# RWKV attention ahead of two expert layers on one Trainium2 core: attention tiles taken in pairs from tile 8 on

## The chip, the cores and the metric

The kernel runs on one core of a Trainium2 chip. The metric is the device time of one execution in microseconds (us); the kernel before and the changed one are compared by the median of their runs.

## The reference

Three layers follow each other. The first is a recurrence over 768 time steps (4 batches, 8 heads, head size 48), the other two are expert layers over 3072 tokens of 384 features.

```python
for t in range(S):
    cur = np.einsum('bhd,bhe->bhde', u[None] * kt, vt)
    y[:, :, t] = np.einsum('bhd,bhde->bhe', rt, state + cur)
    state = w[None, :, :, None] * state + np.einsum('bhd,bhe->bhde', kt, vt)
...
h = np.maximum(np.maximum(x @ w1, x @ w2), x @ w3); x = h @ w_out
...
silu(xn @ w_gate) * (xn @ w_val) @ w_out      # xn: x by its root mean square
```

## The kernel before, in words

**Tiles and stages.** The recurrence is worked in 24 attention tiles: tile i is 128 time steps of one batch (i % 4), 8 heads at once. Four tiles make one block of 512 tokens, the width of an expert matmul. The program is a list of stages `u` = 0 to 5 (the loop `for u in range(NB)`); stage u runs the first expert layer on block u and beside it the attention of block u+1, so tiles 8 to 11 belong to stage 1. A stage is a row of slots: in stages 1 to 4 there are 18 slots of `a_l1` (nine matmuls of 128x512, three each for three weight parts; after the slot VectorE takes a maximum, L537, or ScalarE a copy, L534) and 6 of `a_out` (nine matmuls). Stage 0 has 30 slots.

**One attention tile** is: `prep` (L321, VectorE multiplies the tile `raw` by decay tables; two products `ru`, from tile 8 on by GpSimd), `prep_b` (L337, a sum on VectorE; L340, GpSimd makes the diagonal matrix `Dg`), `pe_a` (L357, 16 matmul records into two PSUM banks `pa`), `mix` (L364, two predicated copies on VectorE from `pa` into `Dg`), `pe_y` (L431, the outputs `py`), `fin` (L446 and L447 split `py` into two halves of a float, from tile 8 on partly through a tile `yt` that `turn` moves between partitions with four DMAs), `pe_st` (L395, `pkv`) and `state` (L375 and L380). The profile counts matmuls of 4-byte numbers as several records.

**Order of the work.** Each engine takes its instructions in the order in which the program issues them. `att_steps` yields 72 steps for the attention. The slot loop issues a slot, then the work put off by the slot before (`later`), then as many steps as `want` asks, evenly over the slots; then `tick` issues pieces of the weights' conversion (L137 to L140 on ScalarE, L147 and sums L168 on VectorE). Up to tile 11 a step is `(scores(i + 1), outputs(i))`, that is `pe_a` and `mix` of the next tile and then `pe_y`, `fin`, `pe_st` of this one, followed by `ahead` (with `prep`) and `ahead_b` (with `prep_b`) of tile i+2. From tile 12 on `outputs` and `scores` each take two tiles at once, in different steps.

**PSUM.** The attention's banks come from the pool `psx`: four banks, given out in turn, each of which must be read before it is given out again. A tile takes four (two `pa`, `py`, `pkv`), a pair seven (four `pa`, two `py`, one `pkv`). One more is taken in stage 1: behind slot 8 `decay_flag` (L301 to L310) issues a small matmul `psok` (L305), whose result on VectorE says whether the decay is in range.

Of the kernel before, what the change touches and what calls it, by code (L numbers as in the profile page):

```python
# [56 lines left out]
FREE = (0, 2, 4, 4, 5, 5, 7, 10, 10)  # L57
TURN = (1, 0, 3)
TURNED = 8
DM, FF1, FF2 = 384, 768, 1536  # L60
NB = S // 128
NT = B * NB
# [9 lines left out]
def rwkv_moe_kernel(ctx, tc, rkT, rkv, wd, ub, cst, rg, w1p, wo1p, w2p, out):  # L72
# [173 lines left out]
    def load_next(n=1):  # L246
        for _ in range(n):
            if loads:
                loads.pop(0)()

    def load_tile(i):
        if i >= NT:
            return
        a = raws[i % 3][:, :, 0:512].rearrange("p s (q t) -> p s q t", t=128)
        t = tp.tile([128, VO + NP * 144], F32, tag="tm", bufs=3, name=f"tm{i}")
        raw_t[i], tm_t[i] = a, t
        for j in range(2):
            loads.append(lambda j=j: sync.dma_start(a[64 * j:64 * j + 48], rkT[i, 48 * j:48 * j + 48]))
        rk = t[:, 0:2 * KO].rearrange("p (s n) -> p s n", s=2)[:, :, 0:DM]
        loads.append(lambda: sync.dma_start(rk, rkv[i, :, 0:2 * DM].rearrange("p (s n) -> p s n", s=2)))  # L260
        loads.append(lambda: sync.dma_start(t[:, VO:], rkv[i, :, 2 * DM:]))
# [61 lines left out]
    def prep(i):  # L323
        prep_raw(i)
        s = st[i]
        tm = s["tm"]
        ru = tp.tile([128, DM], F32, tag="ru", name=f"ru{i}")
        eng = dve if i < NRU else pool
        eng.tensor_tensor(out=ru, in0=tm[:, 0:DM], in1=usb, op=ALU.mult)
        eng.tensor_tensor(out=ru, in0=ru, in1=tm[:, KO:KO + DM], op=ALU.mult)  # L330
        s["ru"] = ru

    def prep_b(i):
        s = st[i]
        a8 = tp.tile([128, H], F32, tag="a8", bufs=2, name=f"a8{i}")
        ru = s["ru"]
        dve.tensor_reduce(out=a8, in_=ru.rearrange("p (h d) -> p h d", d=D), op=ALU.add,  # L337
                          axis=mybir.AxisListType.X)
        Dg = tp.tile([128, H, 128], F32, tag="Dg", bufs=2, name=f"Dg{i}")
        pool.affine_select(out=Dg, in_=a8.unsqueeze(2).to_broadcast([128, H, 128]),  # L340
                           pattern=[[0, H], [1, 128]], channel_multiplier=-1, base=0,
                           compare_op=ALU.is_equal, fill=0.0)
        s["Dg"] = Dg

    def prep2(i):
        if i // B < NB - 1:
            k = st[i]["tm"][:, KO:KO + DM]
            pool.tensor_tensor(out=k, in0=k, in1=kt, op=ALU.mult)

    def pe_a(i):  # L350
        s = st[i]
        raw = s["raw"]
        pa = [psx.tile([128, NP, 128], F32, tag="x", name=f"pa{i}_{j}") for j in range(2)]
        for pr in range(NP):
            for j in range(2):
                sl = slice(64 * j, 64 * j + 48)
                pe.matmul(pa[j][:, pr], raw[sl, 1, pr], raw[sl, 0, pr], start=True, stop=True)  # L357
        s["pa"] = pa

    def mix(i):  # L360
        s = st[i]
        dg = s["Dg"].rearrange("p (r j) t -> p r j t", j=2)
        for j in range(2):
            dve.copy_predicated(out=dg[:, :, j], mask=cmask.unsqueeze(1).to_broadcast([128, NP, 128]),  # L364
                                data=s["pa"][j])
# [17 lines left out]
    def pe_st(i, pk=None):  # L383
        s = st[i]
        c, b = divmod(i, B)
        if c == NB - 1:
            return
        tm = s["tm"]
        v3 = tm[:, VO:].rearrange("p (r q e) -> p r q e", q=3, e=D)
        if pk is None:  # L390
            pk = psx.tile([128, NP, D], F32, tag="x", name=f"pkv{i}")
        for pr in range(NP):
            for j in range(2):
                o = KO + 96 * pr + 48 * j
                pe.matmul(pk[64 * j:64 * j + 64, pr], tm[:, o:o + 64], v3[:, pr, 2 * j], start=True, stop=True)  # L395
        s["pk"] = pk

    def state(i):
        c, b = divmod(i, B)
        if c == NB - 1:  # L400
            return
        pk = st[i]["pk"]
        decay(i)
        if i >= B:
            later.append(lambda: state_in(i, pk))
        else:
            state_in(i, pk)

    def pe_y(i):
        s = st[i]  # L410
        c, b = divmod(i, B)
        tm = s["tm"]
        py = s["py"] = psx.tile([128, 3, 128], F32, tag="x", name=f"py{i}")
        lanes = []
        for n in range(4):
            lane = []
            for k in range(3):
                m = (n + TURN[k] * (i >= TURNED)) % 4
                pr, o = (k, 32 * m) if m < 3 else (3, 32 * k)
                ops = [(tm[:, VO + 144 * pr + 48 * j + o:VO + 144 * pr + 48 * j + o + 32],  # L420
                        s["Dg"][:, 2 * pr + j]) for j in range(2) if o != (64, 0)[j]]
                if c > 0:
                    ops.append((Tst[b][:, pr, o:o + 32], s["raw"][:, 0, pr]))
                for m, (l, r) in enumerate(ops):
                    lane.append((py[32 * n:32 * n + 32, k], l, r, m == 0, m == len(ops) - 1))
            lanes.append(lane)
        for m in range(max(map(len, lanes))):
            for lane in lanes:
                if m < len(lane):
                    o, l, r, start, stop = lane[m]  # L430
                    pe.matmul(o, l, r, start=start, stop=stop)  # L431
# [3 lines left out]
    def fin(i):  # L435
        s = st[i]
        u, m = divmod(i, B)
        if m == 0:
            xt[u] = ap_.tile([128, 2, 3, 512], F32R, tag="x", bufs=2, name=f"x{u}")
        xh, xl = xt[u][:, 0], xt[u][:, 1]  # L440
        o = 128 * m
        cs = slice(o, o + 128)
        y = s["py"]

        def split(hi, lo, y):
            act.copy(hi, y)  # L446
            dve.tensor_tensor(out=lo, in0=y, in1=r32(hi), op=ALU.subtract)  # L447

        if i < TURNED:
            split(xh[:, :, cs], xl[:, :, cs], y)  # L450
            return
        t = tp.tile([128, 2, 2, 128], F32R, tag="yt", bufs=2, name=f"yt{i}")
        split(t[:, 0], t[:, 1], y[:, 0::2])
        split(xh[:, 1, cs], xl[:, 1, cs], y[:, 1])

        def turn():
            for n, k in enumerate((0, 2)):
                o = 32 * TURN[k]
                sync.dma_start(r32(xt[u][o:128, :, k, cs]), r32(t[0:128 - o, :, n]))
                sync.dma_start(r32(xt[u][0:o, :, k, cs]), r32(t[128 - o:128, :, n]))  # L460

        turns.append(turn)
# [3 lines left out]
    def att_steps():  # L466
        def scores(*tiles):
            for i in tiles:
                pe_a(i)
            for i in tiles:  # L470
                mix(i)

        def outputs(*tiles):
            for i in tiles:
                pe_y(i)
            for i in tiles:
                fin(i)
            pk = None
            if len(tiles) > 1 and tiles[0] // B < NB - 1:
                pk = psx.tile([128, 2, NP, D], F32, tag="x", name=f"pkv{tiles[0]}")  # L480
            for n, i in enumerate(tiles):
                pe_st(i, pk if pk is None else pk[:, n])
            for i in tiles:
                state(i)
                load_tile(i + 3)

        def ahead(i):
            while turns:
                turns.pop(0)()
            if i < NT:  # L490
                load_next(2)
                prep(i)

        def ahead_b(i):
            if i < NT:
                load_next(1)
                prep_b(i)
                prep2(i)

        for i in range(11):  # L500
            yield lambda i=i: (scores(i + 1), outputs(i))
            yield lambda i=i: ahead(i + 2)
            yield lambda i=i: ahead_b(i + 2)
        yield lambda: outputs(11)
        yield lambda: ahead(13)
        yield lambda: (ahead_b(13), scores(12, 13))
        for i in range(12, NT, 2):
            yield lambda i=i: (outputs(i, i + 1), load_next(2))
            for j in (i + 2, i + 3):
                yield lambda j=j: ahead(j)  # L510
                yield lambda j=j: ahead_b(j)
            yield lambda i=i: scores(i + 2, i + 3) if i + 2 < NT else None
# [845 lines left out]
```

## Time and profile before

| | us |
|---|---|
| median of 3 runs (809.25 to 812.47) | 811.64 |
| profiled execution | 809.68 |
| its span, first to last instruction | 808.0 |
| TensorE busy in the span | 789.1 |
| VectorE busy in the span | 563.9 |
| ScalarE busy in the span | 420.5 |
| GpSimd busy in the span | 215.3 |

The span is what the trace covers; the profiled execution is 1.7 us longer, for what lies around it. PE in the rows is TensorE, DVE VectorE, ACT ScalarE, POOL GpSimd, SP the engine that issues most DMAs. The mean granted clock of TensorE is 0.993 of full speed. Matmuls overlap, so the distance between the starts of two rows tells what a piece costs, not the duration that a row gives.

### The profile page before, as it was taken

What the parts mean: (1) busy time and instruction counts of PE and PEld (TensorE: products, weight loads), DVE (VectorE), ACT (ScalarE), POOL (GpSimd) and SP (SyncE); (2) the same over time, 40 slices, a digit from 0 to 9 for tenths busy, and PEclk for the clock granted to TensorE, in tenths of its full rate; (3) what the DMA queues carried; (4) which work ended last, traced back from release to release, by engine and by line L of the source; (5) the groups of instructions that cost most, each with busy time, mean ns of one, the idle gap of its engine ahead of it and who ended that gap; (6) DMA issues with size and microseconds to landing.
All of it is one profiled execution on the core that took longest, in us unless ns stands there. A gap on an engine that the chain in (4) does not pass through costs nothing.

```text
span 808.0 us, 14049 instructions
## 1 busy us (share of the span) xinstructions
PE 789.1 (98%) x5090; PEld 651.6 (81%) x5090; DVE 563.9 (70%) x981; ACT 420.5 (52%) x780; POOL 215.3 (27%) x225
## 2 busy tenths in 40 slices
PE   7899999999999999999999999999999999999996
PEld 6788888888888888888788888788888788888885
DVE  8888968749959749418846679856676874655551
ACT  2988864454454452224576675655444555444431
POOL 2486724333533322014368672000000000000000
PEclk9999999999999999999999999999999999999998
DMA  8986786666667733244289874328454405554211
GB/s 236 309 255 183 233 246 203 192 208 204 181 194 220 215 129 94 66 155 144 82 275 331 280 239 154 116 75 278 139 181 138 140 17 175 159 154 139 77 40 43
DMA packets 83738, 139.28 MB, mean 172 GB/s; under 512 B 10566, under 2 KB 47046, under 8 KB 83660
## 3 DMA queue, kind: packets, MB, share of 16 engines
q1 hardware_dynamic: 79964, 121.97, 49.9%
q0 software_dynamic: 3200, 15.73, 5.0%
q8 instruction: 42, 0.69, 0.4%
q10 hardware_dynamic: 496, 0.59, 0.3%
q14 instruction: 36, 0.29, 0.1%
HBM read 98.65 MB, written 35.41 MB: 166 GB/s over the span
## 4 chain that ended last, share of the span: by engine, by line
PE 94%; DVE 2%; ACT 2%; DMA 1%; issue 0%; POOL 0%; SPq 0%; POOLq 0%
PE px L99 11%; PE px L100 11%; PE px L101 11%; PE pl L99 9%; PE pl L100 9%; PE pl L101 9%; PE pa L100 5%; PE pa L101 5%; PE pa L99 5%; PE py L431 5%; PE po L99 3%; PE po L101 3%; PE po L100 3%; PE pa L357 3%; PE pkv L395 1%; PE pw L639 1%
## 5 line engine op out<-in xcount | busy, mean ns | idle before, releaser
L99 PE MATMUL pl<-x,w_a 128*128 128x512 f32 (+1 forms) x342 | 131.7, 385 | 0.3 <-ACT x L446 0.3
L100 PE MATMUL pl<-x,w_a 128*128 128x512 f32 (+1 forms) x342 | 129.6, 379 | 0.7 <-DVE x L447 0.7
L101 PE MATMUL pl<-x,w_a 128*128 128x512 f32 (+1 forms) x342 | 129.5, 379 | 0.5 <-POOL w_a L156 0.5
L99 PEld LDWEIGHTS pl<-x,w_a 128*128 128x128 f32 x342 | 64.3, 188 | 13.7 <-ACT x L446 0.9
L101 PEld LDWEIGHTS pl<-x,w_a 128*128 128x128 f32 x342 | 64.3, 188 | 13.0 <-POOL w_a L156 0.8
L100 PEld LDWEIGHTS pl<-x,w_a 128*128 128x128 f32 x342 | 64.3, 188 | 12.6 <-DVE x L447 1.1
L537 DVE TENSOR_TENSOR c<-pl,c 128x512 f32<-128x512 f32 (+1 forms) x76 | 50.0, 657 | 32.7 <-PE pl L101 30.7
L1076 DVE TENSOR_TENSOR px<-px,sb 128x512 f32<-128x512 f32 x56 | 39.1, 699 | 33.0 <-PE px L101 31.5
L539 ACT CAST h1h<-c 128x512 fp32r<-128x512 f32 (+1 forms) x32 | 19.0, 595 | 75.4 <-DVE c L537 75.3
L340 POOL TENSOR_SCALAR_AFFINE_SELECT Dg<-a 128x1024 f32<-128x1024 f32 x24 | 29.2, 1216 | 96.8 <-DVE a L337 79.2
L1064 ACT COPY sb<-px 128x512 f32<-128x512 f32 x63 | 37.0, 587 | 34.2 <-PE px L101 30.5
L700 POOL TENSOR_TENSOR ws<-wsf,ws 128x384 fp32r<-128x384 f32 x40 | 42.3, 1058 | 37.7 <-ACT ws L699 31.0
L100 PE MATMUL px<-hb,wo 128*128 128x512 f32 x132 | 51.5, 391 | 0.2 <-DVE hb L1062 0.2
L99 PE MATMUL px<-hb,wo 128*128 128x512 f32 x132 | 51.6, 391 | 0.0
L101 PE MATMUL px<-hb,wo 128*128 128x512 f32 x132 | 51.4, 389 | 0.0
L147 DVE SCALAR_TENSOR_TENSOR wf<-wf,wraw 128x384 uint32<-128x384 uint32 x60 | 42.4, 711 | 6.4 <-ACT wraw L140 6.0
L137 ACT ACTIVATE wf<-wraw 128x384 f32<-128x384 f32 x60 | 33.4, 557 | 14.7 <-DMA w2o<-wf 8.8
L431 PE MATMUL py<-Dg,tm 128*32 128x128 f32 x768 | 40.4, 287 | 0.0
L1100 DVE TENSOR_TENSOR hb<-h,hb 128x512 fp32r<-128x512 f32 x36 | 24.9, 692 | 21.8 <-ACT hb L1099 21.6
L139 ACT ACTIVATE wraw<-wraw 128x384 uint16<-128x384 uint32 x60 | 38.8, 647 | 1.9
L140 ACT ACTIVATE wraw<-wf 128x384 f16<-128x384 f32 x60 | 38.7, 646 | 1.9
L431 PEld LDWEIGHTS py<-Dg,tm 128*32 128x32 f32 x768 | 33.7, 114 | 4.5 <-issue 2.9
(306 smaller groups left out, 2063.7 us busy)
## 6 DMA issues: line engine op xcount, KB each, us to landing
ws<-w2s SPq DMA_DIRECT2D x80, 384.0 KB, 3.1
w2s<-ws POOLq DMA_DIRECT2D x40, 384.0 KB, 3.8
wraw<-in_w2p SPq DMA_DIRECT2D x36, 384.0 KB, 6.3
raw<-in_rkT SPq DMA_DIRECT2D x48, 192.0 KB, 4.7
tm<-in_rkv SPq DMA_DIRECT2D x24, 384.0 KB, 4.6
wsf<-w2f SPq DMA_DIRECT2D x120, 64.0 KB, 3.4
tm<-in_rkv SPq DMA_DIRECT2D x24, 288.0 KB, 5.1
wraw<-in_w1p SPq DMA_DIRECT2D x18, 384.0 KB, 7.0
```

What stands on the lines that cost most here:

```text
L99: pe.matmul(o, lh, rh, start=start, stop=False, **kw)
L100: pe.matmul(o, lh, rl, start=False, stop=False, **kw)
L101: pe.matmul(o, ll, rh, start=False, stop=stop, **kw)
L137: act.activation(w, hi.bitcast(F32), AF.Copy, scale=2.0 ** -112)
L139: act.activation(x[:, :, 0], lo, AF.Copy, scale=2.0 ** -29 * (1 - 2.0 ** -12), bias=-0.4996)
L140: act.activation(x[:, :, 1].bitcast(F16), w, AF.Copy)
L147: dve.scalar_tensor_tensor(out=wu, in0=wu, scalar=3, in1=cbits(n).bitcast(U32), op0=ALU.logical_shift_left, op1=ALU.bitwise_or)
L431: pe.matmul(o, l, r, start=start, stop=stop)
L537: dve.tensor_tensor(out=c1[:, :n], in0=p[:, :n], in1=c1[:, :n], op=ALU.max)
L700: pool.tensor_tensor(out=t[:, :, 1], in0=r, in1=r32(t[:, :, 0]), op=ALU.subtract)
L1064: (act.copy if kind == "e" else dve.tensor_copy)(get(ks[1]), get(ks[0]))
L1076: dve.tensor_tensor(out=o, in0=a, in1=b, op=op)
```

## The change

The number 12, from which tiles go in pairs, becomes a constant `PAIRED` = 8, and the three places that were written for 12 follow from it. Tiles 8 and 9 and tiles 10 and 11 are now pairs. The number of steps stays 72 and the slots in which steps are issued stay; only what a step holds is other.

```diff
+PAIRED = 8
...
-        for i in range(11):
+        for i in range(PAIRED - 1):
             yield lambda i=i: (scores(i + 1), outputs(i))
             yield lambda i=i: ahead(i + 2)
             yield lambda i=i: ahead_b(i + 2)
-        yield lambda: outputs(11)
-        yield lambda: ahead(13)
-        yield lambda: (ahead_b(13), scores(12, 13))
-        for i in range(12, NT, 2):
+        yield lambda: outputs(PAIRED - 1)
+        yield lambda: ahead(PAIRED + 1)
+        yield lambda: (ahead_b(PAIRED + 1), scores(PAIRED, PAIRED + 1))
+        for i in range(PAIRED, NT, 2):
             yield lambda i=i: (outputs(i, i + 1), load_next(2))
```

**TensorE at the end of stage 0.** Before, the scores of tile 9 (`pa9`) stand in stage 1, behind its first slot (`pl1_0_0`) and ahead of the outputs of tile 8:

```order
L99 MATMUL pl1_0_0_0_1382<-x1_704,w_a0_290 128x512
L100 MATMUL pl1_0_0_0_1382<-x1_704,w_a0_290 128x512
L101 MATMUL pl1_0_0_0_1382<-x1_704,w_a0_290 128x512
L357 MATMUL pa9_0_1394<-raw0_95 128x128 [waits DMAHW2_49,PE_49]
L357 MATMUL pa9_1_1395<-raw0_95 128x128 [waits DMAHW4_49,PE_49]
L357 MATMUL pa9_0_1394<-raw0_95 128x128
```

Now they stand in stage 0, behind those of tile 8 and ahead of the second slot of the output product (`po0_1`, five slots before stage 1):

```order
L358 MATMUL pa8_0_1240<-raw2_97 128x128
L358 MATMUL pa8_1_1241<-raw2_97 128x128
L358 MATMUL pa9_0_1250<-raw0_95 128x128 [waits DMAHW2_49,DVE_49,PE_49]
L358 MATMUL pa9_1_1251<-raw0_95 128x128 [waits DMAHW4_49,PE_49]
L358 MATMUL pa9_0_1250<-raw0_95 128x128
L358 MATMUL pa9_1_1251<-raw0_95 128x128
L358 MATMUL pa9_0_1250<-raw0_95 128x128
L358 MATMUL pa9_1_1251<-raw0_95 128x128
L358 MATMUL pa9_0_1250<-raw0_95 128x128
L358 MATMUL pa9_1_1251<-raw0_95 128x128
L100 MATMUL po0_1_1271<-h1h0_376,w_o0_1037 128x512 [waits Activation_49]
```

Six slots earlier, `pa9` names a wait for VectorE (DVE) that it did not need to name before. The scores of tile 8 moved from three slots earlier, where they stood ahead of the outputs of tile 7, to this place.

**TensorE in stage 1, at the flag's matmul.** Before, `psok` stands between two slots (`pl1_2_2` and `pl1_3_0`):

```order
L99 MATMUL pl1_2_2_0_1678<-x1_704,w_a2_495 128x512
L100 MATMUL pl1_2_2_0_1678<-x1_704,w_a2_495 128x512
L101 MATMUL pl1_2_2_0_1678<-x1_704,w_a2_495 128x512
L305 MATMUL psok_1695<-small_87,csb_85 1x4 [waits DVE_49]
L305 MATMUL psok_1695<-small_87,csb_85 1x4
L99 MATMUL pl1_3_0_0_1702<-x1_704,w_a3_623 128x512 [waits Activation_49]
```

Now the scores of tiles 10 and 11 stand between that slot and `psok`:

```order
L358 MATMUL pa11_0_1692<-raw2_97 128x128
L358 MATMUL pa11_1_1693<-raw2_97 128x128
L358 MATMUL pa11_0_1692<-raw2_97 128x128
L358 MATMUL pa11_1_1693<-raw2_97 128x128
L306 MATMUL psok_1706<-small_87,csb_85 1x4 [waits DVE_49]
L306 MATMUL psok_1706<-small_87,csb_85 1x4
L100 MATMUL pl1_3_0_0_1713<-x1_704,w_a3_623 128x512 [waits Activation_49]
```

The pool's turn now gives `psok` the bank that held `pa10_0`, the first of the four banks that were just written.

**VectorE at the same place.** Before, the sum of tile 11 and the flag's reduction (`nok`) come behind the two maxima of the slots:

```order
L537 TENSOR_TENSOR c11_2_0_1633<-pl1_2_1_0_1667,c11_2_0_1633 128x512 [waits PE_49,Activation_49]
L537 TENSOR_TENSOR c11_2_0_1633<-pl1_2_2_0_1678,c11_2_0_1633 128x512 [waits DVE_49,PE_49]
L337 TENSOR_REDUCE a811_1690<-ru11_1645 128x8 [waits Pool_49]
L307 TENSOR_REDUCE nok_1698<-psok_1695 1x1 [waits PE_49]
L309 CAST okflag_1700<-nok_1698 1x1 [waits DVE_49]
```

Now the four copies of `mix` for tiles 10 and 11 stand there:

```order
L538 TENSOR_TENSOR c11_2_0_1633<-pl1_2_1_0_1659,c11_2_0_1633 128x512 [waits PE_49,Activation_49]
L538 TENSOR_TENSOR c11_2_0_1633<-pl1_2_2_0_1670,c11_2_0_1633 128x512 [waits DVE_49,PE_49]
L365 COPY_PREDICATED Dg10_1574<-csb_85,pa10_0_1682 128x4x128 [waits PE_49]
L365 COPY_PREDICATED Dg10_1574<-csb_85,pa10_1_1683 128x4x128 [waits PE_49]
L365 COPY_PREDICATED Dg11_1638<-csb_85,pa11_0_1692 128x4x128 [waits PE_49,Pool_49]
L365 COPY_PREDICATED Dg11_1638<-csb_85,pa11_1_1693 128x4x128 [waits PE_49]
L308 TENSOR_REDUCE nok_1709<-psok_1706 1x1 [waits PE_49]
```

The first of them is the one that reads `pa10_0`, whose bank `psok` takes next. Line numbers after the change are one higher.

## Rows read from the trace of the kernel before

**Rows 1.** The page's part 1: busy time, share and instructions by engine
```profile
PE 789.1 (98%) x5090; PEld 651.6 (81%) x5090; DVE 563.9 (70%) x981; ACT 420.5 (52%) x780; POOL 215.3 (27%) x225
```

**Rows 2.** Timeline of PE, tile 9 and outputs 8: start us, us, engine, operation, count
```profile
106.66 1.16 PE L357 MATMUL pa<-raw 48*128 48x128 f32 x16
107.75 0.52 PE L431 MATMUL py<-Dg,tm 128*32 128x128 f32 x9
...
109.42 0.67 PE L395 MATMUL pkv<-tm 128*64 128x48 f32 x16
110.02 0.50 PE L99 MATMUL pl<-x,w_a 128*128 128x512 f32 x1
```

**Rows 3.** Timeline of PE in stage 2, outputs of the pair 12 and 13
```profile
172.02 0.52 PE L431 MATMUL py<-Dg,tm 128*32 128x128 f32 x9
...
175.21 1.14 PE L395 MATMUL pkv<-tm 128*64 128x48 f32 x32
...
176.28 0.50 PE L99 MATMUL pl<-x,w_a 128*128 128x512 f32 x1
```

**Rows 4.** Timelines of PE and DVE in stage 2, scores and mix of 14 and 15
```profile
193.32 2.06 PE L357 MATMUL pa<-raw 48*128 48x128 f32 x32
195.31 0.50 PE L99 MATMUL pl<-x,w_a 128*128 128x512 f32 x1
...
178.71 0.69 DVE L537 TENSOR_TENSOR c<-pl,c 128x512 f32<-128x512 f32 x1 [1.09 <-POOL ru L330]
...
197.51 2.58 DVE L364 COPY_PREDICATED Dg<-csb,pa 128x512 f32<-128x512 uint32 x4
```

**Rows 5.** Timeline of PE in stage 1, at the flag's matmul
```profile
130.09 0.39 PE L100 MATMUL pl<-x,w_a 128*128 128x512 f32 x1
130.31 0.39 PE L101 MATMUL pl<-x,w_a 128*128 128x512 f32 x1
130.63 0.24 PE L305 MATMUL psok<-small,csb 128*1 128x4 f32 x4
```

**Rows 6.** Timelines of PE, ACT and DVE at the end of stage 0
```profile
84.29 1.16 PE L357 MATMUL pa<-raw 48*128 48x128 f32 x16
...
94.33 0.39 PE L99 MATMUL po<-h1h,w_o 128*128 128x512 f32 x1
...
93.10 0.48 ACT L155 CAST w_o<-wf 128x384 fp32r<-128x384 f32 x1
...
94.15 1.89 DVE L321 TENSOR_TENSOR raw<-raw,qk 128x1024 f32<-128x1024 f32 x1
```

**Rows 7.** Timelines of PE and DVE, the same place in stages 3 and 4
```profile
256.19 2.06 PE L357 MATMUL pa<-raw 48*128 48x128 f32 x32
...
260.33 2.59 DVE L364 COPY_PREDICATED Dg<-csb,pa 128x512 f32<-128x512 uint32 x4
...
318.01 2.06 PE L357 MATMUL pa<-raw 48*128 48x128 f32 x32
...
319.20 2.56 DVE L364 COPY_PREDICATED Dg<-csb,pa 128x512 f32<-128x512 uint32 x4 [0.39 <-PE pa L357]
```

**Rows 8.** Timelines of PE and DVE, first slots of stages 1 and 2
```profile
104.53 0.39 PE L99 MATMUL pl<-x,w_a 128*128 128x512 f32 x1
...
169.89 0.39 PE L99 MATMUL pl<-x,w_a 128*128 128x512 f32 x1
...
114.57 0.68 DVE L537 TENSOR_TENSOR c<-pl,c 128x512 f32<-128x512 f32 x1
```

**Rows 9.** Windows (busy by engine, granted clock, DMA), and two PE pauses
```profile
15.00:18.60 3.60, 3.60 (x44) 2.84 (x43) 2.33 (x5) 0.00 (x0) 1.93 (x2) 0.53 1.07 258
...
22.00:25.00 3.00, 3.00 (x36) 2.22 (x33) 2.31 (x4) 2.87 (x6) 2.02 (x2) 0.50 1.04 344
...
20.93 1.51 PE L357 MATMUL pa<-raw 48*128 48x128 f32 x16 [1.74 <-issue]
...
48.11 1.14 PE L357 MATMUL pa<-raw 48*128 48x128 f32 x15 [1.03 <-issue]
```

## The prediction

> **What bounds the kernel.** I read the page's part 1 first: TensorE is busy for 98% of the span, VectorE for 70% [rows 1]. The reader should see there that a matmul taken away or a pause put in moves the end almost one for one, and that work on another engine costs only where TensorE comes to wait for it. Next I read TensorE's timeline around one attention tile by itself [rows 2] and around a pair [rows 3, 4], since the change turns four tiles of the first kind into two of the second. What to see is the distance between the starts of the pieces. Then I read the timelines of VectorE and ScalarE at the two places where the order of TensorE changes: the end of stage 0 [rows 6], and the place behind slot 8 of a paired stage, where stages 2, 3 and 4 already do what stage 1 is to do [rows 4, 7]. Last come the windows with the granted clock [rows 9].
>
> **What the change saves on TensorE.** One tile by itself costs 107.75 - 106.66 = 1.09 us for the scores, 109.42 - 107.75 = 1.67 for the outputs and 110.02 - 109.42 = 0.60 for the state's product, together 3.36 [rows 2]. A pair costs 195.31 - 193.32 = 1.99 [rows 4], 175.21 - 172.02 = 3.19 and 176.28 - 175.21 = 1.07 [rows 3], together 6.25. Two tiles by themselves are 6.72, so a pair saves 0.47, and two pairs save 0.94. No matmul goes away; what goes is the change from one shape to another between pieces. The number of times that TensorE leaves the big matmuls for attention stays: from the scores of tile 8 to those of tiles 12 and 13 it was six times (8 with outputs 7, 9 with 8, 10 with 9, 11 with 10, outputs 11, scores 12 and 13) and is six now (outputs 7, scores 8 and 9, outputs, scores, outputs, scores). The flag's matmul is the exception. By itself its way in takes 130.63 - 130.31 = 0.32 [rows 5], where two big matmuls start 130.31 - 130.09 = 0.22 apart; behind the scores that way in is shared, 0.1 less. Together the saving is 1.0 us. It is certain, and it is small.
>
> **What it adds at the end of stage 0.** The scores of tile 9 now follow those of tile 8 six slots earlier, and need the product `raw` of tile 9 from VectorE. Before, TensorE came to this place at 94.33 [rows 6]. It now comes 1.09 earlier, since the scores of tile 8 no longer stand at 84.29 [rows 6]; with 0.1 for the way in and 1.0 for tile 8's half of a pair it wants tile 9 at 94.33 - 1.09 + 0.1 + 1.0 = 94.3. The product ran from 94.15 and took 1.89, so it ended at 96.04 [rows 6]: a wait of 1.7 us. Could VectorE be earlier? The two copies of `mix` for tile 8 leave its queue ahead of the product; at 2.58 / 4 = 0.65 each [rows 4] that is 1.3, and would leave a wait of 0.4. I take 1.7, because the work just ahead of the product needs a cast by ScalarE that begins only at 93.10 [rows 6], and nothing leaves ScalarE's queue. Bounds 0.4 and 1.7. Behind `raw`, the copies for tiles 8 and 9 now hold VectorE until GpSimd has made `Dg` of tile 9; what is queued behind them is conversion and sums of weights for later stages, which no matmul of stage 0 or 1 reads.
>
> **What it adds in stage 1.** `psok` now stands behind four freshly written banks and takes the first of them, so TensorE waits there until VectorE has made the first copy for tile 10, and all of stage 1 behind `psok` waits with it. Nothing in the trace of before does this, so I bound it by the same place in the later stages, which have the same order on VectorE but no `psok`. In stage 2 the four copies start at 197.51, and the first is done 2.58 / 4 = 0.65 later, at 198.16. The scores give TensorE back at 195.31 [rows 4]. A matmul that waited there would have waited 2.85 us. In stage 3 it is 260.33 + 0.65 against 256.19 + 1.99, 2.8 us; in stage 4 it is 319.20 + 0.64 against 318.01 + 1.99, no wait [rows 7]. Stages 2 and 3 still convert weights beside attention, stage 4 has little of it there; stage 1 is like stages 2 and 3. It even starts later: VectorE reaches its first maximum 114.57 - 104.53 = 10.0 us after the stage's first matmul, in stage 2 178.71 - 169.89 = 8.8 [rows 8, 4]. Stage 1 now has a second tile to split before that maximum, and TensorE comes later by the first wait; I take these two to cancel, and add the 1.2 to 2.85: 4.1 us. A part of it may show one slot earlier, where a slot waits for the bank that the maximum reads; the sum is the same. Bounds 0 (stage 4) and 4.1.
>
> **What a pause does to the clock.** Early in the trace TensorE ran with pauses, and from 15 to 18.6 us the granted clock was 0.53, from 22 to 25 us 0.50: the lower of its two levels, 1.2 GHz instead of 2.4. The second fall came about a microsecond after a pause of 1.74 us in a stretch with little other work. A pause of 1.03 us between dense matmuls, at 48 us, was followed by full clock [rows 9]. A stay of 3.6 us at half speed loses about 3.6 x 0.47 = 1.7 us of work. A pause of some 4 us is longer than any of these, so I add one fall behind `psok`, 1.7, with bounds 0 and 3.4 (one behind each pause). The Trainium skill, "TensorE: Matmul & The Clock Gate", Part 1, says that the throttled clock is the default and that activity releases it; by that rule the change costs more than its waits, 6.5 instead of 4.8, and the early windows agree with it.
>
> **What moves at no cost.** The loads of the next tiles and the four DMAs of each tile's `turn` move by up to three steps on SyncE's queue, and GpSimd's `Dg`, `ru` and decays with them. Their numbers stay. The pairs of stage 2 run with the same distances between load, `turn` and use, and TensorE's rows there show no idle time [rows 3, 4]. That is their cover; if a load landed late, the scores of tile 11 would be next to wait.
>
> **The sum.** -1.0 + 1.7 + 4.1 + 1.7 = +6.5 us against the profiled execution's 809.68, so 816.2. The median of the runs shown is 1.96 above that execution; on it the forecast is 811.64 + 6.5 = 818.1, which I give as 818.
>
> **The rivals.**
> - *The waits come, the clock holds.* 1.7 + 4.1 - 1.0 = +4.8, 816.4; with stage 2's price instead of stage 1's later start, 1.7 + 2.85 - 1.0 = +3.5, 815.2. For it: the pause at 48 us. Against it: that one was a quarter as long.
> - *VectorE is caught up at `psok`.* As in stage 4 the first copy ends before the scores do, and only the wait at tile 9 is left: 1.7 - 1.0 = +0.7, 812.3. For it: the first wait gives VectorE 1.7 us to catch up. Against it: stages 2 and 3 lie 2.8 us behind.
> - *Not slower: both waits are covered.* The mechanism is VectorE's place in its queue: if the raw product moves up by 1.7 us and the copies of tile 10 by some 4, TensorE runs through and only the saving is left: -1.0, 810.6. It decides at the point where VectorE's first copy ends within 1.99 us of the start of the scores. For it: fewer items stand ahead of the product in stage 0. Against it: ScalarE's cast at 93.10, and the rows of stages 2 and 3.
>
> That the change does not do what it says can be left out: the order shows the pairs.
>
> **How the numbers follow.** About 0.5%, 4.1 us, is what a measurement of this kernel can tell from no change: 807.6 to 815.7. The forecast has a chance of 0.47, and its time lies above that band. Waits with a full clock have 0.24, of which 0.15 above the band. The caught-up case has 0.14 and the covered case 0.10, both inside. Some 0.05 is for what I do not see, 0.03 of it faster by over 0.5% (no case gives that) and 0.02 for still slower. So faster 0.03, same 0.33, slower 0.64. The range goes from 812, which leaves out the covered case, to 821, which takes in two falls of the clock (+8.2, 819.8) and a microsecond of scatter; about 0.18 is left out.
>
> **What would show it.** In the profile after: pieces of 1.99, 3.19 and 1.07 us for pairs 8/9 and 10/11; idle time of about 1.7 us inside the scores of tiles 8 and 9, ended by `raw` of VectorE; idle time of some 4 us at `psok` or in part a slot earlier, ended by VectorE's copy into `Dg` or its maximum; granted clock near 0.5 for some microseconds behind it; and the rest of the program moved as a block. The forecast is wrong if `psok` starts with the end of the scores, if the clock stays at full speed, or if TensorE gets the lost time back in a later stage, for which I see no slack, since it hardly waits for anything there.

## The result, and the profile after

| | before | after |
|---|---|---|
| median of 6 runs each, us | 811.68 (809.25 to 815.55) | 819.55 (818.91 to 822.88) |
| profiled execution, us | 809.68 | 819.3 |
| its span, us | 808.0 | 817.6 |
| mean granted clock of TensorE | 0.993 | 0.983 |

The changed kernel takes 1.0114 times as long, with a 95% interval of 1.0096 to 1.0133: 9.3 us more (7.8 to 10.8). The two medians lie 7.9 us apart, at the lower end of that interval. The forecast was 818.0, in a range from 812 to 821.

The page's part 1 of the changed kernel, which answers to [rows 1]:

```profile
PE 793.2 (97%) x5090; PEld 655.1 (80%) x5090; DVE 566.6 (69%) x981; ACT 421.1 (52%) x780; POOL 214.6 (26%) x225
```

TensorE has the same 5090 records. It is busy 4.1 us longer and the span has grown by 9.6: about half of the loss is work that ran slower, and half is time in which TensorE stood still. The waits of TensorE from 90 to 150 us say where it stood still (us in total, times, longest):

```profile
PE psok L306 <- DVE Dg L365: 3.4, 1, 3.4
PE pa L358 <- issue: 1.6, 1, 1.6
```

There are two places and no third. TensorE's timeline at both, and between them the outputs of the pair 8 and 9:

```profile
76.66 0.50 PE L100 MATMUL pl<-x,w_a 128*128 128x512 f32 x1
...
94.09 1.16 PE L358 MATMUL pa<-raw 48*128 48x128 f32 x16
96.86 1.97 PE L358 MATMUL pa<-raw 48*128 48x128 f32 x16 [1.60 <-issue]
98.76 0.79 PE L100 MATMUL po<-h1h,w_o 128*128 128x512 f32 x1
...
109.96 0.39 PE L100 MATMUL pl<-x,w_a 128*128 128x512 f32 x1
...
112.09 0.43 PE L432 MATMUL py<-Dg,tm 128*32 128x128 f32 x8
...
115.28 1.14 PE L396 MATMUL pkv<-tm 128*64 128x48 f32 x32
116.35 0.50 PE L100 MATMUL pl<-x,w_a 128*128 128x512 f32 x1
...
133.66 2.06 PE L358 MATMUL pa<-raw 48*128 48x128 f32 x32
139.13 0.24 PE L306 MATMUL psok<-small,csb 128*1 128x4 f32 x4 [3.42 <-DVE Dg L365]
139.31 0.80 PE L100 MATMUL pl<-x,w_a 128*128 128x512 f32 x1
139.90 0.63 PE L101 MATMUL pl<-x,w_a 128*128 128x512 f32 x1
140.32 0.63 PE L102 MATMUL pl<-x,w_a 128*128 128x512 f32 x1
```

The outputs of the pair cost 115.28 - 112.09 = 3.19 and its state product 116.35 - 115.28 = 1.07, as pairs do in stage 2 [rows 3]. The scores of 8 and 9 took 98.76 - 94.09 = 4.67 us where a pair takes 1.99 [rows 4]. `psok` starts 139.13 - 133.66 = 5.47 behind the start of the scores of 10 and 11, where they alone need 1.99. Behind `psok` two big matmuls start 140.32 - 139.90 = 0.42 us apart, where [rows 5] have 0.22. VectorE at the same two places:

```profile
94.87 1.88 DVE L322 TENSOR_TENSOR raw<-raw,qk 128x1024 f32<-128x1024 f32 x1
...
119.57 0.69 DVE L538 TENSOR_TENSOR c<-pl,c 128x512 f32<-128x512 f32 x1
...
136.97 1.48 DVE L538 TENSOR_TENSOR c<-pl,c 128x512 f32<-128x512 f32 x2
138.36 2.54 DVE L365 COPY_PREDICATED Dg<-csb,pa 128x512 f32<-128x512 uint32 x4
```

`raw` of tile 9 ends at 94.87 + 1.88 = 96.75, and the scores of tile 9 start 0.11 later. The first of four copies into `Dg` is done at 138.36 + 2.54 / 4 = 139.0, and `psok` starts 0.13 later. The windows around both places (the number behind the five engines is the granted clock):

```profile
95.00:97.00 2.00, 0.40 (x8) 0.23 (x5) 2.00 (x2) 1.94 (x5) 0.67 (x1) 1.00 1.00 395
97.00:101.00 4.00, 4.00 (x22) 3.36 (x23) 3.78 (x7) 3.87 (x8) 3.44 (x3) 0.57 0.41 123
101.00:110.00 9.00, 9.00 (x42) 7.41 (x41) 6.31 (x22) 5.06 (x10) 0.05 (x1) 1.00 0.42 118
...
138.00:139.00 1.00, 0.00 (x0) 0.00 (x0) 1.00 (x3) 0.52 (x1) 0.00 (x0) 0.57 1.06 390
139.00:144.00 5.00, 4.87 (x15) 3.87 (x16) 3.14 (x8) 0.55 (x2) 0.00 (x0) 0.50 0.55 176
144.00:145.00 1.00, 1.00 (x3) 0.73 (x3) 0.00 (x0) 0.97 (x3) 0.00 (x0) 0.51 0.00 0
145.00:146.00 1.00, 1.00 (x6) 0.75 (x4) 0.00 (x0) 0.90 (x2) 0.00 (x0) 1.00 0.00 0
```

The clock fell at both pauses. At tile 9 the window behind the restart has 0.57. At `psok` the fall came inside the pause: the window from 138 to 139, in which TensorE did nothing, has 0.57 already, and with levels of 1.00 and 0.50 that puts the fall at about 138.1. The 18 big matmuls behind `psok` took 6.92 us instead of the 4.30 that they take at full clock (run 1), 2.6 lost. The 54 behind the scores of tile 9 took 13.33 instead of 12.47 (run 12), and the scores themselves 0.9 longer: 1.8 lost.

**Two marks inside the program.** The first 75 us differ between the profiles of this document by up to 5 us, though no run changes anything there. So I also compare the stretch between two marks, within which all lies that the change moves: the first big matmul behind the state product of tile 6, and the first behind that of tiles 12 and 13. Before it goes from 75.89 to 176.28 [rows 3], 100.39 us; after, from 76.66 to 185.76, 109.10 us: +8.7. The pieces give -1.0 for the pairs, +1.7 and +1.8 for the pause at tile 9 and the slow stretch behind it, +0.3 in the slots ahead of `psok`, +3.5 and +2.6 for the pause there and what follows: +8.9. From the second mark to the end it is 631.7 before and 631.8 after.

### The profile page after: what moved, and what is told of

The parts are those of the page before. It is cut to its first block, busy times and chain, and to the rows that moved or that the text cites. A ratio compares the mean times of both kernels' runs of the same rounds, so it can differ in the third digit from the quotient of the medians.

```text
span 817.6 us, 14049 instructions
## 1 busy us (share of the span) xinstructions
PE 793.2 (97%) x5090; PEld 655.1 (80%) x5090; DVE 566.6 (69%) x981; ACT 421.1 (52%) x780; POOL 214.6 (26%) x225
## 4 chain that ended last, share of the span: by engine, by line
PE 89%; DVE 5%; DMA 2%; issue 1%; ACT 1%; POOL 1%; SPq 0%; DVEq 0%; POOLq 0%; ACTq 0%
PE px L100 10%; PE px L101 10%; PE px L102 10%; PE pl L100 9%; PE pl L102 8%; PE pl L101 8%; PE pa L101 5%; PE pa L102 5%; PE pa L100 5%; PE py L432 5%; PE po L100 3%; PE po L102 3%; PE po L101 3%; PE pa L358 3%; PE pkv L396 1%
## 5 line engine op out<-in xcount | busy, mean ns | idle before, releaser
L100 PEld LDWEIGHTS pl<-x,w_a 128*128 128x128 f32 x342 | 65.0, 190 | 14.0 <-ACT x L447 0.6
L102 PEld LDWEIGHTS pl<-x,w_a 128*128 128x128 f32 x342 | 64.9, 190 | 13.2 <-POOL w_a L157 0.8
L101 PEld LDWEIGHTS pl<-x,w_a 128*128 128x128 f32 x342 | 65.1, 190 | 12.1 <-DVE x L448 0.4
L148 DVE SCALAR_TENSOR_TENSOR wf<-wf,wraw 128x384 uint32<-128x384 uint32 x60 | 40.3, 678 | 8.2 <-ACT wraw L141 7.8
```

The lines of the kernel that those rows point to most:

```text
L100: pe.matmul(o, lh, rh, start=start, stop=False, **kw)
L101: pe.matmul(o, lh, rl, start=False, stop=False, **kw)
L102: pe.matmul(o, ll, rh, start=False, stop=stop, **kw)
L148: dve.scalar_tensor_tensor(out=wu, in0=wu, scalar=3, in1=cbits(n).bitcast(U32), op0=ALU.logical_shift_left, op1=ALU.bitwise_or)
```

## The experiments

My theory was that the loss is the two waits and the slow clock behind each. The main rivals were that the flag costs something wherever it stands, that the clock falls for another reason than the pauses, and that a wait taken away at one place comes back at the other. Each run has its own measurement of the kernel before on the same chip (medians 810.46 for runs 1 to 4, 810.89 for 5 to 8, 810.19 for 9 to 12). "As us" is the ratio less 1, times that median; intervals in us in the text are worked out from the 95% intervals in the same way. "Between the marks" is that stretch in the run's profile, less the 100.39 of before.

| run | median, us | ratio to before, 95% | as us | between the marks, us |
|---|---|---|---|---|
| the change | 819.55 | 1.0096 to 1.0133 | +9.3 | +8.7 |
| 1 flag at slot 4 | 813.62 | 1.0024 to 1.0054 | +3.2 | +2.8 |
| 2 `raw` of 9 earlier, outputs 7 later | 819.65 | 1.0091 to 1.0131 | +9.0 | +10.0 |
| 3 both | 813.64 | 1.0031 to 1.0066 | +4.0 | +1.7 |
| 4 pairs from 10 | 813.96 | 1.0027 to 1.0057 | +3.4 | +3.7 |
| 5 pause at the flag filled | 816.73 | 1.0056 to 1.0083 | +5.6 | +6.8 |
| 6 before, flag at slot 4 | 811.23 | 0.9988 to 1.0014 | +0.1 | 0.0 |
| 7 `raw` of 9 earlier alone, flag at slot 4 | 811.54 | 0.9994 to 1.0022 | +0.6 | +1.3 |
| 8 `raw` of 9 earlier alone | 817.71 | 1.0062 to 1.0089 | +6.2 | +6.9 |
| 9 pairs from 10, flag at slot 4 | 810.31 | 0.9987 to 1.0010 | -0.2 | -0.4 |
| 10 as 7, one conversion later | 809.50 | 0.9978 to 1.0006 | -0.6 | -1.0 |
| 11 before, one conversion later | 809.80 | 0.9986 to 1.0011 | -0.2 | 0.0 |
| 12 flag at slot 4, pause at tile 9 filled | 812.09 | 1.0012 to 1.0033 | +1.9 | +1.2 |

**Run 1.** The flag's matmul goes behind slot 4, away from the banks that were just written.

```diff
-                if u == 1 and n == 8:
+                if u == 1 and n == 4:
```

> The changed kernel, with the flag's matmul psok behind slot 4 of stage 1 instead of slot 8, so that it takes a bank that VectorE has long read. Theory (two waits of TensorE and the falls of the clock behind them): the 3.4 us at psok, the 0.3 us of slot 8 and the 2.6 us of slow matmuls behind go, the wait at tile 9 (1.6 us and 1.8 us of slow work) stays: +2.4 us against the kernel before, about 814. Rival (pairs in stage 1 are dear by themselves, whatever psok waits for): still about +8, 819.

TensorE's timeline there, two slots that run through:

```profile
123.74 0.39 PE L102 MATMUL pl<-x,w_a 128*128 128x512 f32 x1
124.06 0.24 PE L306 MATMUL psok<-small,csb 128*1 128x4 f32 x4
124.23 0.50 PE L100 MATMUL pl<-x,w_a 128*128 128x512 f32 x1
```

`psok` no longer waits, and between the marks 5.9 us of the 8.7 are back. What is left is tile 9: the scores took 3.96 us, and 54 big matmuls behind them 14.09. The time, +3.2 us (1.9 to 4.4), leaves out the rival's +8.

**Runs 2 and 3.** `raw` of tile 9 is made before the outputs of tile 7 are issued; run 3 has run 1's edit as well.

```diff
-        yield lambda: outputs(PAIRED - 1)
         yield lambda: ahead(PAIRED + 1)
+        yield lambda: outputs(PAIRED - 1)
```

> The changed kernel, with the step that prepares tile 9 put ahead of the outputs of tile 7 instead of behind them, two slots earlier, so that the product raw of tile 9 is done when the scores ask for it. Theory: the pause of 1.6 us inside the scores of tiles 8 and 9 goes, and the slow work behind it (1.8 us) with it; psok stays: +5.3 us against the kernel before, about 817. Rival (the pairs are dear by themselves): still about +8, 819.

> Both of the edits of the two kernels before this one. Theory: TensorE runs through as before the change and only the saving of the pairs is left, -1.0 us against the kernel before, about 810.7, with pieces of 1.99, 3.19 and 1.07 us for the pairs 8/9 and 10/11 and no idle time of TensorE in stage 1. Rival (the pairs are dear by themselves): well above the kernel before.

Both missed: +9.0 us where +5.3 was expected, and +4.0 where it was -1.0. By the times alone the rival, that pairs are dear by themselves, could be right here; runs 7 to 10 decide against it. In run 3 (and run 2 alike) TensorE still waits inside the scores of tiles 8 and 9:

```profile
95.04 1.16 PE L358 MATMUL pa<-raw 48*128 48x128 f32 x16
96.72 0.48 PE L358 MATMUL pa<-raw 48*128 48x128 f32 x2 [0.53 <-DMA wraw<-in_w2p]
98.66 1.13 PE L358 MATMUL pa<-raw 48*128 48x128 f32 x14 [1.45 <-issue]
```

and VectorE shows that it is no longer `raw` that is late:

```profile
89.61 1.90 DVE L322 TENSOR_TENSOR raw<-raw,qk 128x1024 f32<-128x1024 f32 x1
...
96.13 0.54 DVE L448 TENSOR_TENSOR x<-py,x 128x384 fp32r<-128x384 f32 x1
...
97.83 0.73 DVE L376 SCALAR_TENSOR_TENSOR T<-pkv,csb,T 128x192 f32<-128x192 f32 x2
```

`raw` is ready at 91.5. What ends at 96.67 and at 98.56 is VectorE's reading of `py` and `pkv` of tile 7, and the scores of tile 9 go on 0.05 and 0.10 us later: they take those two banks next. My edit had moved the outputs of tile 7 two slots back, so their banks came free later. The page names a DMA and "issue" here, and both names mislead; the times of the ends do not.

**Run 4.** One pair less.

```diff
-PAIRED = 8
+PAIRED = 10
```

> The changed kernel with the pairs from tile 10 on instead of tile 8: stage 0 is that of the kernel before, and the scores of tiles 10 and 11 still stand right ahead of psok. Theory: one pair's saving (-0.5 us), the wait at psok (3.4 to 3.7 us) and the slow work behind it (2.6 us): +5.7 us, about 817.4. Rival (the loss comes with the number of pairs): half of the change's loss, about +4, 815.7.

A wait of 2.85 us at `psok`, and 18 matmuls behind it in 5.86 instead of 4.30. The wait at tile 9 is gone. One pair saves 0.5, the wait adds 2.9 and the slow stretch 1.6: +4.0, and +3.7 is measured between the marks. The expected +5.7 was too much: the flag's wait and the slow stretch were both shorter than I had put them. By the time alone (+3.4, 2.2 to 4.6) the rival's +4 fits better. The trace has the loss at `psok`, though, and run 9, with the same pair and the flag moved, loses nothing.

**Run 5.** Work in place of the pause; the rest of the changed kernel as it is.

```diff
                 if u == 1 and n == 8:
+                    fl = psm.tile([128, 512], F32, tag="m", name="fl")
+                    for _ in range(16):
+                        pe.matmul(fl, wts["a", 0][:, 0, 0:128], xt[1][:, 0, 0], start=True, stop=True)
```

> The changed kernel with 16 extra matmuls of 128x512 ahead of the decay flag's matmuls behind slot 8 of stage 1; their sums go to a bank that nothing reads, so they are work added for this run alone. At 0.227 us each they fill 3.6 us, about the 3.4 us that TensorE waited there. Theory (the clock fell because TensorE stood still at the flag): the wait becomes matmuls of the same length, the flag's matmuls come at nearly the same time, the granted clock stays at 1.00 behind them, and M n18 behind it takes 4.3 instead of 6.9 us: 2.6 us less than the changed kernel, about +6 us on the kernel before (817 to 818 us). Rival (the clock falls there whatever TensorE does in the pause): the slow stretch of some 6 us stays, and the time is that of the changed kernel or some tenths above it (+8.5 to +9).

TensorE's timeline, and its windows:

```profile
135.37 2.06 PE L358 MATMUL pa<-raw 48*128 48x128 f32 x32
137.36 3.96 PE L862 MATMUL fl<-x,w_a 128*128 128x512 f32 x16
141.25 0.24 PE L306 MATMUL psok<-small,csb 128*1 128x4 f32 x4
```

```profile
136.00:141.00 5.00, 5.00 (x42) 4.16 (x40) 4.79 (x10) 2.17 (x4) 1.25 (x2) 1.00 0.60 212
141.00:146.00 5.00, 5.00 (x36) 3.71 (x38) 2.94 (x8) 2.14 (x4) 0.00 (x0) 1.00 0.53 172
```

`psok` comes no earlier, 5.88 us behind the start of the scores, and yet the stretch between the marks is 1.9 us shorter than with the change: the 18 matmuls behind take 4.31 us at full clock, 2.6 less, and the filling costs 0.4 more than the pause did. The median agrees: +5.6 us (4.5 to 6.7) leaves out the rival's +8.5. The slow stretch came from the pause, not from what lies around it. That agrees with the Trainium skill, "TensorE: Matmul & The Clock Gate", Part 1, by which activity is what releases the throttle.

**Run 6.** The control for run 1: the same edit on the kernel before.

> The kernel before with the decay flag's matmuls behind slot 4 of stage 1 instead of slot 8, and nothing else. It is the control for moving the flag. Theory: in the kernel before nothing waits at the flag (its matmuls follow the scores without a pause), so moving it gives nothing: 0, within 0.5 us of the kernel before. Rival: the earlier place is better in itself, by a lighter VectorE or a shorter way in, and then part of what the moved flag gave back in the changed kernel is no cure of the wait: -1 us or more.

No difference: +0.1 us (-1.0 to +1.1). The flag's place alone is worth nothing that can be measured, so what run 1 gave back was the wait and what follows it.

**Runs 7 and 8.** `raw` of tile 9 goes one step earlier, its sum and `Dg` with it, and the outputs of tile 7 stay; run 7 has the flag behind slot 4 as well.

```diff
-        yield lambda: outputs(PAIRED - 1)
-        yield lambda: ahead(PAIRED + 1)
-        yield lambda: (ahead_b(PAIRED + 1), scores(PAIRED, PAIRED + 1))
+        yield lambda: (outputs(PAIRED - 1), ahead(PAIRED + 1))
+        yield lambda: ahead_b(PAIRED + 1)
+        yield lambda: scores(PAIRED, PAIRED + 1)
```

> The changed kernel with the product raw of tile 9 issued one step earlier while the outputs of tile 7 keep their place (so that tile 9's scores find both raw and the banks ready), and with the decay flag behind slot 4. Theory (the change's loss is two waits and the clock falls behind them): with both waits gone the scores of tiles 8 and 9 take 2.0 us again, the flag has no wait, no clock fall follows, and the saving of the pairs alone is left: -1.0 us on the kernel before (about 0.9988). Rival 1 (the saving is used up in stage 1, where the longer run of paired work delays the slots): 0. Rival 2 (tile 9's scores still meet a bank that is freed late): +0.5 to +2.5.

> The changed kernel with the product raw of tile 9 issued one step earlier alone; the decay flag keeps its place behind slot 8. Theory: the wait of 1.6 us at tile 9's scores and the slow stretch behind it (1.8 us) go, the wait at the flag (3.4 us) and the slow stretch behind that (2.6 us) stay: +8.7 - 3.4 = +5.3 us on the kernel before. Rival (the two places are not independent: less delay at the first makes the second wait longer by the same amount, since VectorE's chain sets when the flag is ready): +7 to +9.

In both the scores of 8 and 9 take 1.99 us, with no wait and no fall. And in both a new wait stands in the first slots of stage 1. In run 7:

```profile
125.37 0.39 PE L612 MATMUL ss<-srl,ones 128*128 128x512 f32 x1
126.86 0.50 PE L100 MATMUL pl<-x,w_a 128*128 128x512 f32 x1 [1.10 <-ACT c L535]
...
131.80 0.50 PE L100 MATMUL pl<-x,w_a 128*128 128x512 f32 x1 [0.56 <-DVE c L538]
```

The first two start 1.49 us apart instead of 0.23, 1.26 lost, and the 27 big matmuls behind take 7.23 us where they take 6.24 in run 10, 1.0 lost: with the -1.0 of the pairs that is +1.3, and 1.3 is measured between the marks. Run 8 loses 3.0 us in the same slots, 2.7 more than the change does there, and so gives back most of the 3.5 that it saves at tile 9. It ends 1.8 below the change between the marks because the clock cost 1.0 less behind `psok`. Its time, +6.2 us (5.0 to 7.2), fits its theory's +5.3 and the lower end of its rival's +7 to +9 alike; the wait at `psok` did not grow (3.41), so the time came back at a third place that neither had named. Of run 7's rivals, rival 2 had the size but not the place, and rival 1 the place. The cause can be read from ScalarE and VectorE in run 7:

```profile
114.86 0.56 ACT L138 ACTIVATE wf<-wraw 128x384 f32<-128x384 f32 x1 [0.36 <-issue]
...
116.63 0.56 ACT L535 COPY c<-pl 128x512 f32<-128x512 f32 x1
117.09 0.38 ACT L447 CAST yt<-py 128x256 fp32r<-128x256 f32 x1
...
117.50 0.42 DVE L448 TENSOR_TENSOR yt<-py,yt 128x256 fp32r<-128x256 f32 x1 [3.34 <-ACT yt L447]
...
119.96 0.69 DVE L538 TENSOR_TENSOR c<-pl,c 128x512 f32<-128x512 f32 x1
```

ScalarE reaches the first copy of stage 1 at 116.63, and the splits of tiles 8 and 9 behind it, with a weight conversion of 116.63 - 114.86 = 1.77 us just ahead. VectorE waits for the splits, and makes its first maximum 12.0 us after the stage's first matmul (119.96 - 108.00). In the change it was 119.57 - 109.96 = 9.6, and before 10.0 [rows 8]. The delay at tile 9 had hidden this.

**Run 9.** Pairs from tile 10 on, with the flag behind slot 4 (the edits of runs 4 and 1).

> Pairs from tile 10 on, and the decay flag behind slot 4 of stage 1. Theory: of what pairs from tile 10 on cost (+3.5 us), 2.9 us was the wait at the flag and 1.6 us the slow stretch behind it; with the flag ahead of the pair both go, and the saving of one pair is left: -0.5 to -1.2 us on the kernel before. Rival (time that VectorE and ScalarE no longer get from a wait of TensorE is asked for elsewhere, as at the first slots of stage 1 with pairs from tile 8 on): a new wait of 1 to 2.5 us in stage 1, and +0.5 to +2.

No wait, no fall: the pair's scores take 2.13 us and the big matmuls behind them 4.32. Between the marks it is 0.4 shorter than before, which is one pair's saving. The medians (-0.2 us, -1.1 to +0.8) cannot tell it from before.

**Runs 10 and 11.** Run 10 is run 7 without the weight conversion behind the last slot of stage 0; the later conversions each come one step later, and none is left out. Run 11 has the same edit on the kernel before.

```diff
-U0T = (..., 1, 1, 1, 1)
+U0T = (..., 1, 1, 1, 0)
```

> As raw of tile 9 one step earlier with the flag behind slot 4, and the weight conversion step behind the last slot of stage 0 left out there (the later ones each come one step later). Theory (there TensorE waited 1.49 us behind the sums of squares and 0.94 us more at the next slots, because ScalarE reached the first copy of stage 1 and the splits of tiles 8 and 9 too late, with 1.77 us of a weight conversion just ahead of them): the copy comes about 1.8 us earlier, the first wait goes, the second with it, and the time is -1 us on the kernel before. Rival (what holds the splits is the wait of ScalarE for the store that frees a conversion buffer, or VectorE itself): the waits stay, +1.0 to +1.5.

> The control of the moved weight conversion: the kernel before with the same step left out behind the last slot of stage 0. Theory: nothing in the kernel before waits there, so 0, within 0.5 us. Rival: the later conversions delay something in the later stages (weights of the second matrix, or the catch-up ahead of the last stage), +0.5 to +2; or ScalarE's relief is a gain by itself, -0.5 to -1.

In run 10 ScalarE comes to the copy right behind the stage before:

```profile
112.68 0.59 ACT L567 ACTIVATE sq<-po 128x512 f32<-128x512 f32 x1
113.16 0.58 ACT L535 COPY c<-pl 128x512 f32<-128x512 f32 x1
113.63 0.39 ACT L447 CAST yt<-py 128x256 fp32r<-128x256 f32 x1
```

and TensorE runs through:

```profile
123.70 0.39 PE L612 MATMUL ss<-srl,ones 128*128 128x512 f32 x1
123.93 0.39 PE L100 MATMUL pl<-x,w_a 128*128 128x512 f32 x1
```

The first maximum is at 116.56, 10.2 us after the stage's first matmul at 106.33. Both waits are gone; it was ScalarE's queue. Between the marks the run is 1.0 us shorter than before, which is the saving of two pairs, and run 11 is equal to before. By the medians neither run differs from before, so that pairs from tile 8 on with all three cures beat the kernel before is seen in one profile and not shown by the times.

**Run 12.** Run 1 with the pause at tile 9 filled.

```diff
             for i in tiles:
+                if i == PAIRED + 1:
+                    fl = psm.tile([128, 512], F32, tag="m", name="fl")
+                    for _ in range(7):
+                        pe.matmul(fl, wts["a", 0][:, 0, 0:128], xt[0][:, 0, 0], start=True, stop=True)
                 pe_a(i)
```

> The changed kernel with the decay flag behind slot 4, and 7 extra matmuls of 128x512 (1.6 us, into a bank that nothing reads) between the scores of tile 8 and those of tile 9, where TensorE waited 1.6 us. Theory (the slow stretch of 1.6 us behind those scores comes from TensorE's standing still): the granted clock stays at 1.00 behind them, M n54 takes 12.5 instead of 14.1 us. If the two places simply add, the time is then 1.6 us under the run with the flag moved alone: +0.6 us on the kernel before. If the splits of tiles 8 and 9 limit stage 1 (as with raw of tile 9 earlier), some 0.4 us of it come back as a wait at its first slots: +1.0. Rival (the clock falls there for another reason, the dense work before): M n54 still takes 13.3 to 14.1 us, and the time is +2 to +2.7.

TensorE's timeline and its window behind:

```profile
96.30 1.89 PE L473 MATMUL fl<-x,w_a 128*128 128x512 f32 x7
98.12 1.16 PE L358 MATMUL pa<-raw 48*128 48x128 f32 x16
99.21 0.50 PE L100 MATMUL po<-h1h,w_o 128*128 128x512 f32 x1
```

```profile
97.00:101.00 4.00, 4.00 (x30) 3.08 (x29) 3.78 (x7) 3.87 (x8) 2.70 (x3) 1.00 0.70 249
```

The clock stays at 1.00, and 54 matmuls take 12.47 us instead of run 1's 14.09. In this profile the fall is gone with the pause. The times don't settle it: +1.9 us (1.0 to 2.7) leaves out the first case (+0.6), but holds both the second case (+1.0) and the rival's +2 to +2.7. And in run 3 the clock held at this place behind pauses that were not filled. So that the pause brings the fall at tile 9 is likely, and less firmly shown than at `psok` (run 5). Between the marks it is +1.2, near the second case. The 0.4 us that were to come back at stage 1's first slots are not there as a wait, though (the slots behind `ss` lose 0.2); the filling was 0.2 longer than the pause.

## Why the prediction was right

**The direction and the mechanism** were right: two waits, at `raw` of tile 9 and at `psok`, and a slow clock. The time was 1.5 us above the forecast and inside the range. That it came so near is in part luck: the forecast of +6.5 stands against +8.7 between the marks, and against +9.6 in the profiled execution (816.2 forecast, 819.3 measured). The median shown before lies 2.0 us above its profiled execution, that of the change only 0.25, and that difference hid part of the error.

**The saving of 1.0.** The pieces are as forecast, 1.99, 3.19 and 1.07 us, and runs 9 and 10, in which nothing waits, come out 0.4 and 1.0 shorter between the marks, for one pair and for two.

**The wait at tile 9**, put at 1.7, was 1.60. The forecast took the upper bound because a cast by ScalarE and not the removed copies sets VectorE's time there. The engine was right and the item was another: VectorE waited 1.30 us for ScalarE's split of tile 7's outputs (until 90.02, about as long as the two copies had taken), and less than 0.1 for the cast. Measured from the first mark, `raw` started 0.05 us earlier than before, so the copies that left the queue gave nothing.

**The wait at `psok`**, put at 4.1, was 3.42, and 0.3 more in the slots ahead of it. The prediction took the second split and the later TensorE "to cancel". They did, nearly: the first maximum came 9.6 us after the stage's first matmul, 0.4 sooner than before, and 12.4 in run 8, where TensorE was not late (119.53 - 107.17). With 9.6 in place of 10.0 the prediction's own sum gives 3.7, which is what the wait and those slots cost.

**The step that was mis-sized** is the clock: "I add one fall behind `psok`, 1.7, with bounds 0 and 3.4". There were two falls, 1.8 and 2.6 us, together 4.4 and so above the upper bound. Two things went wrong. The pause of 1.03 us at 48 us [rows 9], behind which the clock held, spoke for the pause at tile 9 as well; that one was 1.60, and behind it the clock fell. And the size came from an early stay of 3.6 us, while the stay at `psok` lasted from about 138.1 to 145.0, 6.8 us, 5.9 of them with TensorE at work. The `psok` wait (0.3 less with the slots ahead of it) and the clock (2.7 more) account for the difference between the forecast of +6.5 and the +8.7 between the marks.

**The rivals.** That the clock holds fell with the windows. That VectorE is caught up at `psok` fell with the 3.42. That both waits are covered is what run 10 does, but only after three edits.

**The rest of the program** moved as a block, as forecast: it takes the same 631.7 to 631.8 us behind the second mark, and nothing was got back.

## What to carry to other kernels

The saving of a pair is 0.47 us, seen in the profiles and too small for the medians; the price is that its scores come earlier and fill all four banks at once, so whoever takes the next bank, even a matmul of four columns, inherits a wait. Before merging steps on the engine that bounds, ask for each merged piece which bank it takes and what reads that bank last. Where the clock fell, a pause of the bounding engine cost 1.5 times its length (run 8, 5.1 us for 3.41) to 3 times (run 2 at tile 9, 5.9 for 1.97), and where it held 1.4 times (run 3, 2.7 for 1.98). A wait that is cured by itself can come back at the next place (run 8): look who had caught up during the pause.

## What the runs showed of the hardware that I had not expected

- The clock fell from 1.00 to 0.50 behind a pause of only 1.60 us (the change, and runs 1 and 5 with 1.62), in a stretch where TensorE was busy nearly all the time ahead of it. With two pauses of 0.52 and 1.45 us at the same place it fell in run 2 (54 matmuls in 14.81 us), and with 0.53 and 1.45 us it held at 1.00 in run 3 (12.48 us): the length of the pause alone does not decide. What does stays open.
- Equal pauses do not cost the same. Behind 3.42 us at `psok` the change lost 2.6 us, behind 3.41 run 8 lost 1.6 (18 matmuls in 5.93 us). In run 8 the pause ended at 139.09 and the clock fell behind it, from 140.0 to 143.4; in the change it fell a microsecond before the pause ended and stayed low until 145.0. Why is open. Run 8's windows:

```profile
139.00:140.00 1.00, 0.91 (x7) 0.78 (x8) 1.00 (x3) 0.06 (x1) 0.00 (x0) 1.00 1.01 369
140.00:143.40 3.40, 3.40 (x9) 2.64 (x9) 2.10 (x6) 0.49 (x2) 0.00 (x0) 0.50 0.49 146
```

- The first 75 us differ by microseconds from profile to profile: the mark lies at 75.89 in that of before and at 81.05 in that of run 9, though nothing ahead of it was changed. The clock falls there at other places each time, but that is not all of it: its mean ahead of the mark is 0.96 before, 0.89 in run 9, and 0.89 in run 3 too, whose mark lies at 77.62.
